# One gate multiply from GpSimd to VectorE behind a layer norm, and batch norm shifts issued among the statistics

## The chip, the cores and the metric

The kernel runs on one core of a Trainium2 chip. The metric is the device time of one execution in microseconds (us); lower is better. Times of whole executions spread over about 1 us and more from one execution to the next. So a second measure is used throughout, read from the traces: **the length of the passage**, from the first matmul of the first pointwise convolution behind attention to the first matmul of the second feed-forward block. All that the change touches lies in there.

## The reference, cut to what matters

A conformer block over x of 2 x 4000 tokens and 512 features: a feed-forward block, attention, a convolution module, a second feed-forward block, a last layer norm. The passage holds the end of attention and the convolution module:

```python
x2 = x1 + attn
h = _layernorm(x2, axis=-1)
h = h @ w_pw1
a = h[..., :D].copy()
b = h[..., D:].copy()
h = a * _sigmoid(b)                       # the gate
hp = jnp.pad(h, ((0, 0), (pad, K - 1 - pad), (0, 0)))
dc = jnp.zeros_like(h)
for i in range(K):                        # depthwise convolution, K = 3
    dc = dc + hp[:, i:i + T, :] * dw[i][None, None, :]
flat = dc.reshape(-1, D)                  # batch norm over ALL tokens
mu = flat.mean(0)
var = ((flat - mu) ** 2).mean(0)
dc = (dc - mu[None, None, :]) / jnp.sqrt(var[None, None, :] + 1e-05)
h = _silu(dc) @ w_pw2
x3 = x2 + h
```

The batch norm's mean and variance run over all 8000 tokens, so nothing of the second feed-forward block can start before the last chunk of tokens has left attention and gone through layer norm, pointwise convolution, gate, depthwise convolution and statistics. That makes the passage a chain.

## The kernel before

Tokens are worked in 16 chunks of 500 (`NCK`), four tiles of 125 in a chunk, features in 4 blocks of 128 (`DC`). `last` is chunk 15, `tail` is chunk 14. `KEEP` is 1. Most chunks' convolutions run beside attention; the passage does the rest. The gate of chunk `tail`:

```python
def conv_a(self, t, jj):
    ps, b_ps = self.pw1(t, jj)
    k, gs = jj % 2, t % 2
    out = self.G[gs][:, jj, 1:1 + CHUNK]
    wr = [self.b_G[gs][jj], self.b_Gl[gs][jj], self.b_Gr[gs][jj]]
    if t == NCK - 2 and jj >= self.KEEP:
        asb, b_asb = self.asb[jj % 3], self.b_asb[jj % 3]
        self.act(asb, ps[:, 0:CHUNK], AF.Copy, [b_ps], [b_asb], scale=2.0)

        def gate(eng):
            self.S.op(eng, lambda e: e.tensor_tensor(out=out, in0=asb, in1=self.th[k], op=ALU.mult), ...)
            self.halo_left(t, jj)          # one-column copies, on GpSimd
            self.halo_right(t, jj)

        if jj < DC - 1:
            return gate("POOL")
        return lambda: gate("DVE")
    elif t == NCK - 1:
        self.halo_left(t, jj)
        self.S.op("DVE", lambda e: e.scalar_tensor_tensor(...), ...)     # gate from PSUM
    # ... (the other chunks, and halo_right)
```

The layer norm that runs between, tile by tile. `ln_factor` ends with a power on GpSimd; `finish` prepares ScalarE's shift with a one-column instruction on VectorE, which is the profile's L620:

```python
def ln_tiles(self, c, sl, prepare=None, engs=("ACT", "ACT", "ACT", "DVE"), src=None):
    def finish(ti):
        if engs[ti] == "ACT":
            S.op("DVE", lambda e: e.scalar_tensor_tensor(               # L620
                out=self.sh[sl][:, ti:ti + 1], in0=self.mv[sl][:, ti, 0:1], scalar=-1.0,
                in1=self.rs[sl][:, ti:ti + 1], op0=ALU.mult, op1=ALU.mult), ...)
        self.ln_norm(c, sl, ti, self.ltm[ti][0:TILE, :], self.b_ltm[ti], engs[ti], src)

    for ti in range(TPC):
        if prepare:
            prepare(ti)
        if ti:
            self.ln_mean(sl, ti - 1)
        self.ln_stats(c, sl, ti, src)
        if ti:
            self.ln_factor(sl, ti - 1)
        if ti > 1:
            finish(ti - 2)
            yield ti - 2
    # ... (the last two tiles)
```

`depthwise(t, cc)` issues three matmuls into a PSUM bank and returns two functions: the statistics on VectorE (L1048) and the copy on ScalarE. `conv_scale(cc)` aggregates a block's statistics on VectorE (L1055) and takes the power on GpSimd (L1057); `conv_shift(cc)` multiplies mean and scale on VectorE (L1062); `swish` applies both on ScalarE. All waits are semaphores, placed by a helper that tracks each buffer's writers and readers. The order of the calls in the passage is shown in the diff below.

## Time and profile before

| | before |
|---|---|
| time, three first executions | 2060.94, 2061.27, 2062.01 us |
| span of the profile | 2056.9 us |
| TensorE busy | 2044.4 us (99%) |
| VectorE / ScalarE / GpSimd busy | 1111.3 / 744.6 / 128.1 us |
| length of the passage (1526.44 to 1564.25) | 37.81 us |
| TensorE idle in the passage | 0.95 + 0.23 + 0.12 + 0.85 + 0.32 + 0.87 = 3.34 us |

TensorE is the engine that sets the time, so only its idle times can be won. The prediction calls three of them gap A (0.95), gap B (0.23) and gap C (0.85) and says what each waits for.

### The profile page before, as it was taken

To read this page: it belongs to the slowest core of one execution; us is meant where nothing else is said; L and a number is where in the kernel's file an instruction comes from. 1 tells how busy PE (TensorE), PEld (TensorE's weight loads), DVE (VectorE), ACT (ScalarE), POOL (GpSimd) and SP (SyncE) were. 2 spreads that over 40 slices of the span, in tenths; PEclk is the share of its full clock that TensorE was granted. 3 is DMA by queue.
4 is the path that set the end of the run, shared out by engine and by line. 5 is a ranking of instruction groups with operands and counts; after the bars stand their busy time and mean duration, and the time that the engine had idled before them with its cause. 6 is when DMAs were issued, how large, how long until landed. Compare 5 with 4: busy or idle time off the path is not lost.

```text
span 2056.9 us, 24335 instructions
## 1 busy us (share of the span) xinstructions
PE 2044.4 (99%) x9625; PEld 1036.1 (50%) x9625; DVE 1111.3 (54%) x2274; ACT 744.6 (36%) x1270; POOL 128.1 (6%) x275
## 2 busy tenths in 40 slices
PE   9999999999999999999999999999999999999998
PEld 4555555554444444444444444444445555555554
DVE  4245444325556667666666676667764443443443
ACT  3433333333333333333333333333345443443432
POOL 2011100000000000000000000000011000000000
PEclk9999999999999999999999999999999999999999
DMA  7222221110000100014301000101143111111111
GB/s 178 56 61 56 58 61 49 46 49 11 16 6 23 24 16 18 21 23 110 92 17 24 18 23 14 23 18 24 39 127 93 31 31 41 31 31 41 31 31 42
DMA packets 209323, 87.71 MB, mean 43 GB/s; under 512 B 157873, under 2 KB 208692, under 8 KB 209204
## 3 DMA queue, kind: packets, MB, share of 16 engines
q1 hardware_dynamic: 208808, 85.79, 16.7%
q8 instruction: 77, 1.26, 0.3%
q14 instruction: 42, 0.34, 0.1%
q10 hardware_dynamic: 396, 0.31, 0.0%
HBM read 29.53 MB, written 19.04 MB: 24 GB/s over the span
## 4 chain that ended last, share of the span: by engine, by line
PE 96%; DVE 2%; SPq 1%; DMA 1%; issue 0%; POOL 0%; ACT 0%; POOLq 0%; DVEq 0%; ACTq 0%
PE s L465 54%; PE y L465 42%; SPq L515 1%; DMA xt<-in_x_dram 1%; DMA work<-in_dw_dram 0%; DVE work L547 0%; SPq L511 0%; DVE work L569 0%; DVE wff L1048 0%; DVE xt L667 0%; SPq L519 0%; POOL work L661 0%; POOL work L1057 0%; DVE wff L953 0%; ACT work L507 0%
## 5 line engine op out<-in xcount | busy, mean ns | idle before, releaser
L507 ACT ACTIVATE work<-s 128x500 bf16<-128x500 f32 (+2 forms) x1063 | 623.7, 587 | 1220.4 <-PE s L465 1218.9
L465 PE MATMUL s<-work,wff 128*128 128x500 bf16 x2560 | 627.7, 376 | 1.7 <-DVE work L504 1.7
L465 PE MATMUL s<-work,keys 128*128 128x500 bf16 x2048 | 517.5, 374 | 0.1
L465 PE MATMUL y<-work,keys 128*128 128x500 bf16 x2048 | 514.4, 373 | 0.1
L465 PE MATMUL y<-wff,work 128*125 128x512 bf16 x2016 | 506.6, 379 | 0.0
L820 DVE TENSOR_TENSOR work<-work 128x500 f32<-128x500 f32 x496 | 334.8, 675 | 281.9 <-ACT work L507 279.1
L465 PEld LDWEIGHTS s<-work,wff 128*128 128x128 bf16 x2560 | 250.1, 98 | 280.9 <-issue 1.8
L465 PEld LDWEIGHTS y<-wff,work 128*125 128x125 bf16 x2016 | 275.2, 137 | 173.5
L465 PEld LDWEIGHTS y<-work,keys 128*128 128x128 bf16 x2048 | 199.2, 97 | 234.4 <-DVE work L885 1.1
L465 PEld LDWEIGHTS s<-work,keys 128*128 128x128 bf16 x2048 | 199.8, 98 | 232.2 <-DVE work L749 0.6
L667 DVE SCALAR_TENSOR_TENSOR xt<-y,xt 125x512 bf16<-125x512 f32 x128 | 79.8, 684 | 342.0 <-PE y L465 342.0
L547 DVE BATCH_NORM_STATS2 work<-xt 125x6 f32<-125x512 bf16 x316 | 199.8, 681 | 10.4 <-DMA xt<-in_x_dram 10.2
L556 POOL TENSOR_TENSOR work<-work 125x4 f32<-125x4 f32 x76 | 77.0, 1013 | 1116.6 <-DVE work L554 1116.6
L465 PE MATMUL s<-work 128*125 128x512 bf16 (+3 forms) x528 | 133.7, 378 | 2.2 <-DVE work L1158 1.2
L569 DVE TENSOR_SCALAR work<-xt,work 125x512 bf16<-125x512 bf16 x279 | 113.0, 449 | 16.5 <-POOL work L556 12.9
L667 DVE SCALAR_TENSOR_TENSOR xt<-s,xt 125x512 bf16<-125x512 f32 x56 | 38.8, 692 | 146.3 <-PE s L465 146.3
L465 PEld LDWEIGHTS s<-work 128*125 128x125 bf16 (+2 forms) x528 | 70.5, 135 | 48.1 <-issue 2.7
L667 DVE SCALAR_TENSOR_TENSOR xt<-s,work,xt 125x512 bf16<-125x512 f32 x64 | 48.1, 751 | 32.5 <-PE s L465 31.9
L465 PE MATMUL s<-keys,work 128*128 128x500 bf16 x256 | 64.4, 376 | 0.0
L957 DVE SCALAR_TENSOR_TENSOR wff<-wff,s 128x500 bf16<-128x500 f32 x57 | 38.6, 678 | 43.5 <-PE s L465 41.4
L507 ACT ACTIVATE wff<-s 128x500 f32<-128x500 f32 x67 | 39.2, 587 | 57.2 <-PE s L465 55.1
L507 ACT ACTIVATE work<-keys,work 128x500 bf16<-128x500 bf16 x64 | 50.5, 795 | 1.1 <-DVE work L1062 1.1
(90 smaller groups left out, 491.4 us busy)
## 6 DMA issues: line engine op xcount, KB each, us to landing
xt<-in_x_dram SPq DMA_DIRECT2D x15, 500.0 KB
out_dram<-work SPq DMA_DIRECT2D x15, 500.0 KB
dcvd<-wff SPq DMA_DIRECT2D x52, 125.0 KB, 1.7
keys<-dcvd SPq DMA_DIRECT2D x13, 500.0 KB, 4.3
wff<-in_w_ff_a_dram SPq DMA_DIRECT2D x16, 256.0 KB, 4.7
keys<-work SPq DMA_DIRECT2D x8, 512.0 KB, 3.6
keys<-keys SPq DMA_DIRECT2D x32, 128.0 KB, 2.1
work<-work SPq DMA_TRANSPOSE x210, 2.5
```

The lines of the kernel that those rows point to most:

```text
L465: self.S.op("PE", lambda e: e.matmul(out, lhsT, rhs, start=start, stop=stop), reads=reads, writes=[bank], inc=stop if inc is None else inc)
L507: return self.S.op("ACT", lambda e: e.activation(out, in_, func, **kw), reads=reads, writes=writes)
L515: return self.S.dma("SP", k, lambda e: e.dma_start_transpose(dst, src), reads=reads, writes=writes)
L547: self.S.op("DVE", lambda e: e.bn_stats(self.st[sl][:, ti, :], x), reads=[b_x], writes=[self.b_st[sl][ti]])
L556: S.op("POOL", lambda e: e.tensor_tensor(out=self.rs[sl], in0=self.va[sl], in1=self.neghalf[0:TILE, :], op=ALU.pow), reads=self.b_va[sl] + ...
L569: self.S.op("DVE", lambda e: e.tensor_scalar(out, x, self.mv[sl][:, ti, 0:1], self.rs[sl][:, ti:ti + 1], ALU.subtract, ALU.mult), reads=[b ...
L667: self.S.op("DVE", lambda e: e.scalar_tensor_tensor(out=self.XT[g], in0=ps, scalar=scalar, in1=self.XT[g], op0=ALU.mult, op1=ALU.add), rea ...
L820: S.op("DVE", lambda e, p=p: e.tensor_tensor(out=self.acc[s], in0=self.acc[s], in1=self.P[p], op=ALU.add), reads=[self.b_P[p], self.b_acc[ ...
L957: self.S.op("DVE", lambda e: e.scalar_tensor_tensor(out=out, in0=self.th[k], scalar=1.0, in1=ps[:, 0:CHUNK], op0=ALU.add, op1=ALU.mult), r ...
```

## The change

Its intent: GpSimd is slow at the gate (1.245 us, against 0.672 on VectorE), so block 2's gate goes to VectorE, behind the layer norm, where block 3's already is. The depthwise convolution of chunk 13's block 2 reads what that gate's halo copies write, so it moves behind as well. And the shifts of the batch norm, which VectorE issued ahead of the next block's statistics, are issued between the two statistics.

```diff
@@ -945,7 +945,7 @@
                 self.halo_left(t, jj)
                 self.halo_right(t, jj)
 
-            if jj < DC - 1:
+            if jj < DC - 2:
                 return gate("POOL")
             return lambda: gate("DVE")
         elif t == NCK - 1:
@@ -1275,22 +1275,24 @@
             self.conv_b(tail, jj)
             self.conv_a(tail, jj)
 
+        gates = []
+
         def prepare(ti):
             self.project(last, ti)
             if ti == 0:
                 self.conv_b(tail, DC - 2)
-            if ti == 2:
-                self.conv_a(tail, DC - 2)
+            if ti == 1:
+                gates.append(self.conv_a(tail, DC - 2))
 
         for ti in self.ln_tiles(last, self.nxt("ln", self.LN_SLOTS), prepare, ("ACT", "ACT", "DVE", "DVE")):
             if ti == TPC - 3:
                 self.conv_b(tail, DC - 1)
-                gate = self.conv_a(tail, DC - 1)
+                gates.append(self.conv_a(tail, DC - 1))
         drains = [self.depthwise(tail - 1, self.KEEP)]
         for k in range(2):
             self.transpose_pair(k, 1, ("ACT", "DVE")[k], ybank())
-        drains.append(self.depthwise(tail - 1, DC - 2))
-        gate()
+        for gate in gates:
+            gate()
         self.load(self.Wp2, i["w_pw2"].rearrange("(c p) f -> p c f", p=128), [self.b_Wp2])
         for t in range(6, TCB):
             self.fetch_conv(t)
@@ -1304,6 +1306,8 @@
                 f, copy = self.depthwise(t, cc)
                 f()
                 copies.append(copy)
+                if t == last and cc > 1:
+                    self.conv_shift(cc - 1)
             self.conv_scale(cc)
 
         def copy_away():
@@ -1316,26 +1320,26 @@
                 self.act(self.nr1, self.onef, AF.Silu, [self.b_onef], [self.b_nr1])
             copy_away()
             self.conv_a(last, jj)
-            if jj > 1:
-                self.conv_shift(jj - 2)
+            if jj == 2:
+                self.conv_shift(0)
             if jj:
                 finish(jj - 1)
             else:
-                f, copy = self.depthwise(tail - 1, DC - 1)
-                f()
-                copies.append(copy)
+                for cc in (DC - 2, DC - 1):
+                    f, copy = self.depthwise(tail - 1, cc)
+                    f()
+                    copies.append(copy)
         self.swish(0, 0)
         self.swish(0, 1)
         copy_away()
         clear = (14848 - 12288) // (F // self.NWA * 2)
         for k in range(clear):
             self.load_wa(i["w_ff2_a"], k)
-        self.conv_shift(DC - 2)
-        self.swish(0, 2)
         all_t = range(TPC)
         banks = [self.sbank() for _ in all_t]
         self.pw2_x(0, all_t[0:2], banks[0:2])
         finish(DC - 1)
+        self.swish(0, 2)
         self.conv_shift(DC - 1)
         self.swish(0, 3)
         copy_away()
```

## The prediction

What the text on record said of the hardware that no trace of this case shows is cut from it, and the cuts are marked. The sum came to -0.29 + 0.64 - 0.72 = -0.37 us; L620 goes from 0.74 to 0.15 us once no gate runs on GpSimd beside it. That it does was the author's estimate, from two ends that agree to 0.01 us. The first rival is that GpSimd's gate was not what held L620.

> **What bounds the kernel now.** I first read the engine totals of the page: TensorE (PE) is busy 2044.4 of 2056.9 us, VectorE (DVE) 1111.3, ScalarE (ACT) 744.6, GpSimd (POOL) 128.1. The granted clock is 1.000. A change that moves VectorE and GpSimd work can only win what TensorE idles, 12.5 us in all, most of it at the first loads and the last store. Next come the waits of TensorE over the whole span (engine and line that waited, releaser, total us, times, longest us):
>
> ```profile
> PE s L465 <- DVE work L504: 1.7, 3, 0.9
> PE s L465 <- DVE work L1158: 1.2, 1, 1.2
> PE s L480 <- ACT work L507: 1.1, 2, 0.8
> PE y L493 <- ACT work L507: 1.0, 1, 1.0
> PE s L465 <- ACT work L507: 0.8, 1, 0.8
> PE y L493 <- DVE xt L504: 0.3, 1, 0.3
> ```
>
> L1158 and L480 lie elsewhere (weight folding, head). The rest is to be placed by the timeline of TensorE from 1524 to 1572 us, the passage between attention (its last matmul is at 1526 us) and the second feed-forward block. Its idle times are 0.95, 0.23, 0.85, 0.32 and 0.87 us, besides one of 0.12 us at 1550.8 that is worked out from two neighbouring lines; 3.34 us together. The change's code lies around these three:
>
> ```profile
> 1536.96 1.07 PE L493 MATMUL y<-work 125*128 125x125 bf16 x12 [0.95 <-ACT work L507]
> ...
> 1538.91 1.86 PE L465 MATMUL s<-work,wff 128*128 128x500 bf16 x8 [0.23 <-DVE work L504]
> ...
> 1556.30 1.08 PE L465 MATMUL s<-work 128*125 128x512 bf16 x4 [0.85 <-ACT work L507]
> ```
>
> Gap A (0.95): the transposes of layer-norm tile 1 wait for ScalarE's normalisation. Gap B (0.23): the first pointwise convolution of the last chunk waits for the copy of the transposed tiles. Gap C (0.85): the second pointwise convolution of chunk 0 waits for the last swish. The other two (0.32, 0.87) belong to the layer norm that follows gap C and start from its end, so they move with it.
>
> Why is gap A there? The timeline of all engines around 1534 us (start, us, engine, line, operation):
>
> ```profile
> 1533.29 1.25 POOL L943 TENSOR_TENSOR wff<-wff 128x500 bf16<-128x500 f32 x1 [0.21 <-ACT wff L507]
> ...
> 1533.80 0.74 DVE L620 SCALAR_TENSOR_TENSOR work<-work 125x1 f32<-125x1 f32 x1
> ...
> 1534.58 0.81 ACT L507 ACTIVATE work<-xt,work 125x512 bf16<-125x512 bf16 x1 [1.37 <-DVE work L620]
> ```
>
> L620 works on one column and takes 0.15 us in its other executions (median 151 ns of 7, longest 745). Here it lasts until 1533.80 + 0.74 = 1534.54, and GpSimd's gate multiply lasts until 1533.29 + 1.25 = 1534.54. VectorE stood still some 0.6 us for the gate. It is in the chain that ended last, which runs through VectorE from the third residual (1532.4) to the normalisations.
>
> Why gap C? The chain that ended last, from 1552 us:
>
> ```profile
> 1552.10 0.56 POOL work L1057
> ...
> 1552.75 0.09 DVE work L1062
> 1552.85 0.68 DVE wff L1048
> ...
> 1555.44 0.81 ACT work L507
> ...
> 1556.30 0.44 PE s L465
> ```
>
> L1057 is GpSimd's power for the scale of channel block 2, L1062 its shift on VectorE, L1048 the statistics of block 3. VectorE ended block 2's aggregate at 1552.02, then idled 0.73 us for the power before the shift, with block 3's statistics queued behind it. Block 3's first matmuls (1550.88, three of 0.213 us pitch) had been complete since about 1551.7.
>
> [...]L620 has two SBUF inputs and ends with the gate, while the neighbouring statistics (0.69 us, one SBUF input) and residuals (0.74 us, one input from PSUM) ran beside gates at their usual durations.[...] here the same gate takes 1.245 us on GpSimd and 0.672 us on VectorE, 1.85 times.
>
> **The change part by part.**
>
> 1. *Gate of block 2 from GpSimd to VectorE.* It takes 1.245 us from GpSimd, and adds one VectorE gate of 0.67 us (0.60 from start to start) after the copy of the transposed tiles, beside the gate of block 3 that is there already. [...]L620 goes from 0.74 to 0.15, worth about 0.59 us of VectorE's chain. But block 2's first half now precedes the third projection on TensorE, so that projection goes from about 1530.7 to 1531.58. Its last matmul ends at 1531.58 + 3 x 0.213 + 0.38 = 1532.60, and the residual, which started at 1532.37, starts at about 1532.68: 0.31 late. From there the old steps run: L620 at 1532.68 + 1.43 = 1534.11, the fourth residual at 1534.18 (was 1534.47), L620 of tile 1 at 1535.62 (was 1535.91), the normalisation to 1536.61, the transposes at 1536.67. **Minus 0.29 us**, and everything behind it, up to the copies that end gap B, shifts alike: the last chunk's convolution starts at 1538.62 in place of 1538.91.
>
> 2. *The depthwise of chunk 13's block 2 moves behind that convolution.* It needs the gate that now comes later. Before, its three matmuls filled 3 x 0.213 = 0.64 us between the transposes and gap B. Now TensorE idles there and does them later: gap B becomes about 0.23 + 0.64 = 0.87, and from block 1's convolution on TensorE is at 1538.62 + 1.71 + 1.28 = 1541.61 in place of 1541.26. **Plus 0.64, so plus 0.35 so far.** VectorE can take the gate: copy at 1537.78, gates 1538.38 and 1538.97, statistics to 1540.24; ScalarE's copy and sigmoid to 1541.34; last chunk's gate 0 to 1542.05, two statistics of 0.70 to about 1543.40, and gate 1 must wait for TensorE until about 1543.57 (1543.22 + 0.35). Spare: 0.17 us. From gate 1 on the chain is statistics, aggregate, power, halo copies, next gate, 3.2 us a round (1543.22, 1546.40, 1549.67), above TensorE's 14 x 0.213 = 2.98; it carries the 0.35 through unchanged.
>
> 3. *Shifts among the statistics.* The shift of block 2 now follows the first of block 3's two statistics. With 0.35 of lag: aggregate of block 2 at 1552.12, first statistics at 1552.35 to 1553.05, power ready by 1553.0, shift at 1553.10, second statistics at 1553.18 to 1553.88, aggregate at 1553.92, power at 1554.24, shift at 1554.89, swish 1555.09 to 1555.89, TensorE at about 1555.94 against 1556.30. One instruction of 0.70 now lies in a wait of 0.73: **minus 0.72**. Block 1's shift waits for nothing in either order: zero. The swish of block 2 has its shift at 1553.26 and ends, at 0.81 us, by 1554.1, ahead of its matmuls at 1554.6.
>
> Sum: -0.29 + 0.64 - 0.72 = **-0.37 us**. As gaps: A 0.66, B 0.87, C 0.85 - 0.72 = 0.13 plus what the other signs move; from 3.34 to about 2.97 us in all. No other part of the program changes. 2061.27 - 0.37 = **2060.9 us**.
>
> **Rivals.** [...] Against: both ends agree to 0.01 us. Then part 1 is a loss of 0.31 in place of a win of 0.29, and the sum is +0.23: 2061.5. *VectorE becomes the bound in front of gate 1.* For it: one more gate, and only 0.17 us spare[...]. A delay of 0.3 there goes straight into the chain: 2061.2. *TensorE was not going to need the earlier swish*, because it arrives late itself: its queue reaches the last four matmuls at about 1555.5 in the new schedule, so gap C can shrink by no more than some 0.1 beyond what I take: a floor of about 2060.8. *A loss is possible only* if two of these meet.
>
> **Range and chances.** The mechanism moves the time by -0.5 to +0.3. The three runs of before spread over 1.07 us, so the median of new runs can differ by half a microsecond and more without any cause. Both together give 2059.8 to 2062.2. Two per cent is 41 us, over ten times all TensorE idling in the passage: within 2% is all but certain.
>
> **What would show it right or wrong.** Right: no L620 above 0.2 us in the passage; the only large GpSimd gate at 1529; tile 1's transposes near 1536.7; a TensorE wait of about 0.9 us before the last chunk's convolution near 1538.6; block 1's convolution near 1541.6; no 0.73 us VectorE wait before L1062 of block 2; last swish near 1555.1 and a TensorE wait before it of 0.1 to 0.2. Wrong: a gate 0 or gate 1 delayed beyond TensorE's results (then the second rival), tile 1's transposes later than before (the first), or a swish of block 2 that TensorE waits for.

## The result, and the profile after

| | before | after |
|---|---|---|
| median, first comparison | 2061.34 (4 runs, 2060.94 to 2062.01) | 2060.18 (4 runs, 2059.99 to 2061.96) |
| median, second comparison | 2060.71 (8 runs, 2060.56 to 2061.84) | 2060.13 (5 runs, 2059.82 to 2061.94) |
| ratio, first; second | | 0.9996 [0.9979, 1.0013]; 0.9998 [0.9984, 1.0012] |
| passage | 37.81 us | 37.35 us, and 37.33 in a second trace |

A ratio is the mean time of one kernel's fast runs over that of the other's of the same rounds, so it isn't quite the ratio of the medians. By time alone the two kernels can't be told apart; the traces show the passage 0.46 us shorter. Of the 0.7 us between the two profiled spans (2056.9 and 2056.2), 0.18 is there before the passage starts (1526.44 and 1526.26), in code that the change doesn't touch.

The waits of TensorE in the changed kernel, over the whole span (engine and line that waited, releaser, total us, times, longest us):

```profile
PE s L465 <- DVE work L504: 2.3, 3, 0.9
PE s L465 <- DVE work L1158: 1.3, 1, 1.3
PE s L480 <- ACT work L507: 1.1, 2, 0.8
PE y L493 <- ACT work L507: 0.6, 1, 0.6
PE y L493 <- DVE xt L504: 0.3, 1, 0.3
```

The wait on ScalarE's swish (0.8, gap C) is no longer in the list. The one on the normalised tile (L493 on L507) fell from 1.0 to 0.6, and that on the copies (L504) rose from 1.7 to 2.3: gap C is no longer listed (0.26 us of it is left, which this view hides; see the third rival below), gap A is shorter, gap B longer. TensorE's timeline of the changed kernel places them (start, us, then what, and in brackets the idle time before it with its releaser):

```profile
1536.46 1.07 PE L493 MATMUL y<-work 125*128 125x125 bf16 x12 [0.63 <-ACT work L507]
1538.41 1.86 PE L465 MATMUL s<-work,wff 128*128 128x500 bf16 x8 [0.87 <-DVE work L504]
1540.11 1.43 PE L465 MATMUL y<-wff 128*128 128x500 bf16 x6
1541.37 1.86 PE L465 MATMUL s<-work,wff 128*128 128x500 bf16 x8
...
1552.70 4.04 PE L465 MATMUL s<-work 128*125 128x512 bf16 x16
```

Gap B grew to 0.87 because the three matmuls that used to stand in front of it are now among the six behind the convolution. In the last line all sixteen matmuls of the second pointwise convolution stand together. Before they were twelve and four, 0.85 us apart.

The timeline of all engines around 1534 us, where L620 stood still before:

```profile
1533.90 0.15 DVE L620 SCALAR_TENSOR_TENSOR work<-work 125x1 f32<-125x1 f32 x1
```

L620 is at 0.15 us. And the chain that ended last, at its end in the passage:

```profile
1552.15 0.56 POOL work L1057
...
1552.80 0.06 DVE work L1062
...
1552.91 0.70 DVE wff L1048
...
1554.81 0.81 ACT work L507
```

The same instructions as before, but only one of block 3's two statistics now stands behind the shift (L1062); the other ran while GpSimd worked. The last swish starts at 1554.81 in place of 1555.44.

Two lines of VectorE and GpSimd, taken from their own timelines, show something that cost nothing here but looks like what L620 met in the kernel before. VectorE's two gates:

```profile
1538.18 1.26 DVE L943 TENSOR_TENSOR wff<-wff 128x500 bf16<-128x500 f32 x2
```

and GpSimd's one-column halo copies behind the first of them:

```profile
1538.91 0.57 POOL L1027 COPY wff<-wff 128x1 bf16<-128x1 bf16 x1 [2.27 <-DVE wff L943]
1539.42 0.18 POOL L1037 COPY wff<-wff 128x1 bf16<-128x1 bf16 x1
```

The first copy takes 0.57 us where others take 0.18, and ends at 1539.48, just behind the second gate (1538.18 + 1.26 = 1539.44). It takes 0.57 in the three traces with both gates on VectorE whose list of GpSimd was read there (after, e2, e7), and 0.19 in the kernel before. So a long duration was seen on both sides: L620's 0.74 us beside GpSimd's gate, and this copy's 0.57 beside VectorE's second gate. Both lie in the reported duration and not in the idle time before it.

### The profile page after: what moved, and what is told of

It is laid out like the page before. It is cut to its first block, busy times and chain, and to the rows that moved or that the text cites. A ratio compares the mean times of both kernels' runs of the same rounds, so it can differ in the third digit from the quotient of the medians.

```text
span 2056.2 us, 24336 instructions
## 1 busy us (share of the span) xinstructions
PE 2044.3 (99%) x9625; PEld 1036.2 (50%) x9625; DVE 1112.1 (54%) x2275; ACT 744.7 (36%) x1270; POOL 127.0 (6%) x274
## 4 chain that ended last, share of the span: by engine, by line
PE 98%; DVE 1%; issue 0%; POOL 0%; ACT 0%; DMA 0%; POOLq 0%; SPq 0%; DVEq 0%; ACTq 0%
PE s L465 55%; PE y L465 42%; DVE work L547 0%; ACT work L507 0%; DVE wff L1048 0%; DVE work L569 0%; DMA xt<-in_x_dram 0%; POOL work L661 0%; POOL work L1057 0%; DVE xt L667 0%; DVE wff L953 0%; DVE work L504 0%; DVE work L654 0%; PE y L493 0%; DVE work L1055 0%
## 5 line engine op out<-in xcount | busy, mean ns | idle before, releaser
L507 ACT ACTIVATE work<-s 128x500 bf16<-128x500 f32 (+2 forms) x1063 | 623.8, 587 | 1220.0 <-PE s L465 1218.5
L507 ACT ACTIVATE wff<-s 128x500 f32<-128x500 f32 x67 | 39.2, 587 | 56.7 <-PE s L465 54.6
L507 ACT ACTIVATE work<-keys,work 128x500 bf16<-128x500 bf16 x64 | 50.5, 795 | 0.4 <-DVE work L1062 0.4
```

Of the source, the lines that this page charges most:

```text
L507: return self.S.op("ACT", lambda e: e.activation(out, in_, func, **kw), reads=reads, writes=writes)
```

## The experiments

All twelve runs gave correct results. e1 to e8 were executed once each, so whether they were in the fast state is unknown, and they are read by the passage of their traces and not by their times. Passage lengths, with the prediction for each:

| run | what it is | expected | passage |
|---|---|---|---|
| e1 | part 3 alone | 37.06 | 37.07 |
| e2 | parts 1 and 2 alone | 38.1 | 39.78; 38.10 without a clock drop |
| e3 | before, L620 with one tensor input | 37.35 | 37.35 |
| e4 | after, extra GpSimd multiply over L620 | 37.5 to 37.65 | 37.43 |
| e5 | after, GpSimd fills over L620 | 37.35 | 39.01; 37.33 without a clock drop |
| e6 | e1 and e3 together | 36.6 | 36.60 |
| e7 | after, early halo copies | 36.95 | 37.03 |
| e8 | e1, e3 and early halo copies | 36.2 | 36.28 |
| e9 | after, again | 37.35 | 37.33 |
| e10 | after, gap B filled | 37.35 | 37.33 |
| e11, e12 | e1 and e8, timed | 37.07, 36.28 | 37.04, 36.28 |

### e1: the shifts alone

```diff
 # finish(cc), in the kernel before
                 copies.append(copy)
+                if t == last and cc > 1:
+                    self.conv_shift(cc - 1)
             self.conv_scale(cc)
 # loop over jj
-            if jj > 1:
-                self.conv_shift(jj - 2)
+            if jj == 2:
+                self.conv_shift(0)
 # behind it
-        self.conv_shift(DC - 2)
-        self.swish(0, 2)
 ...
         finish(DC - 1)
+        self.swish(0, 2)
         self.conv_shift(DC - 1)
```

> The kernel before with only the shifts moved among the statistics (part 3). I measure the passage from the first matmul behind attention's last one to the first matmul of the second feed-forward block: 37.81 us before, 37.35 us after. My theory: part 3 is worth 0.75 us by itself, TensorE's wait before the last swish (0.85 us) falls to about 0.1, gaps A and B stay at 0.95 and 0.23: passage 37.06, shorter than the changed kernel's. Rival: the shift only pays together with the moved gate, because TensorE would not yet need the swish: passage 37.6 to 37.8.

Measured: 37.07 us, with gaps A and B at 0.95 and 0.23 as before, and the sixteen last matmuls in one piece of 4.04 us, as in the changed kernel. Part 3 is worth 0.74 us without any help from the moved gate, and by itself gives more than the whole change. The rival falls.

### e2: the moved gate alone

The reverse of e1's diff, applied to the changed kernel.

> The changed kernel with part 3 undone, so only the gate and the depthwise moved. My theory: L620 takes 0.15 us, gap A 0.63, gap B 0.87, gap C stays at about 0.85, so a loss of 0.29: passage 38.1 us against 37.81 before. Rival: the moved gate wins by itself[...]: passage 37.5 or less.

Measured: gaps 0.63, 0.87 and 0.85, L620 at 0.15: as the theory says. But the passage was 39.78 us, and TensorE's timeline shows a line that no other kernel had shown so far:

```profile
1538.85 3.44 PE L465 MATMUL s<-work,wff 128*128 128x500 bf16 x8 [0.87 <-DVE work L504]
```

Eight matmuls that took 1.86 us elsewhere took 3.44. The view by stretches of 1 us (stretch, its length, TensorE busy with its instructions, **granted clock**, share of DMA, GB/s) tells why:

```profile
1538.00:1539.00 1.00, 0.15 (x1) 0.97 1.01 323
1539.00:1540.00 1.00, 1.00 (x3) 0.50 0.92 312
...
1542.00:1543.00 1.00, 1.00 (x5) 0.82 0.00 0
```

From about 1538.95 to 1542.35, 3.4 us, the clock was halved. From the first of those eight matmuls to the next convolution took 4.64 us in this run and 2.96 in the changed kernel: a loss of 1.68. Without it the passage is 39.78 - 1.68 = 38.10, what the theory said (37.81 + 0.29). So the moved gate by itself loses 0.29 us, even though it frees L620. The clock drop is taken up below, with e9 and e10.

### e3: L620 without its second tensor input

```diff
-                S.op("DVE", lambda e: e.scalar_tensor_tensor(
-                    out=self.sh[sl][:, ti:ti + 1], in0=self.mv[sl][:, ti, 0:1], scalar=-1.0,
-                    in1=self.rs[sl][:, ti:ti + 1], op0=ALU.mult, op1=ALU.mult),
+                S.op("DVE", lambda e: e.tensor_scalar(
+                    self.sh[sl][:, ti:ti + 1], self.mv[sl][:, ti, 0:1],
+                    self.rs[sl][:, ti:ti + 1], -1.0, ALU.mult, ALU.mult),
```

> The kernel before, with L620 written as a multiply by two scalars (one SBUF tensor input in place of two); the gate stays on GpSimd and runs beside it. My theory[...]: the instruction takes about 0.15 us although the gate runs, VectorE's chain is 0.59 us earlier, but tile 1's power still stands behind the gate on GpSimd, so gap A goes from 0.95 to about 0.5 and the passage to 37.35 us; gaps B and C stay. Rival (any short VectorE instruction after a scalar factor is held up by a running GpSimd gate, or the instruction waited for something else): it takes 0.74 us again and the passage stays 37.8.

The same product; the scale is now a per-partition scalar and not a second tensor. The timeline around it:

```profile
1533.84 1.25 POOL L943 TENSOR_TENSOR wff<-wff 128x500 bf16<-128x500 f32 x1 [0.21 <-ACT wff L507]
...
1534.35 0.20 DVE L620 TENSOR_SCALAR work<-work 125x1 f32<-125x1 f32 x1
```

The gate ran from 1533.84 to 1535.09, and L620 ran in the midst of it, in 0.20 us (0.21 for tile 1, beside no gate). Gap A went to 0.56 and the passage to 37.35: the same win as the whole change, for one rewritten instruction.

### e4 and e5: GpSimd work over L620 that reads, and that doesn't

```diff
 # prepare(ti), in the changed kernel; e4, then e5
+            if ti == 2:
+                S.op("POOL", lambda e: e.tensor_tensor(out=self.asb[0], in0=self.asb[2], in1=self.th[0], op=ALU.mult), ...)
+            if ti == 2:
+                for _ in range(2):
+                    S.op("POOL", lambda e: e.memset(self.fill, 0.0), ...)     # 1000 fp32, over asb[0] and asb[1]
```

> The changed kernel with an extra gate-sized multiply on GpSimd (result not used) behind tile 0's power, to run at about 1532.9 to 1534.2 of this passage's clock, over L620's time at 1533.9. My theory: L620 lasts until the extra multiply ends, about 0.3 us in place of 0.15, and everything behind moves by 0.15 to 0.3: passage 37.5 to 37.65. Rival ([...]the old gate did harm only by delaying GpSimd's powers): L620 0.15, passage 37.35.

> The changed kernel with two extra fills of 1000 fp32 elements on GpSimd behind tile 0's power, in the same place as the extra multiply of the run before; a fill writes SBUF and reads nothing. [...]L620 takes 0.15 us while a fill runs, passage 37.35. Rival (any GpSimd work holds it): L620 lasts until a fill ends, passage 37.5 or more.

In e4 the extra multiply, at its own line L1282, and L620:

```profile
1533.20 1.24 POOL L1282 TENSOR_TENSOR wff<-wff 128x500 f32<-128x500 f32 x1
...
1534.23 0.23 DVE L620 SCALAR_TENSOR_TENSOR work<-work 125x1 f32<-125x1 f32 x1
```

L620 ended at 1534.46, just behind the multiply (1533.20 + 1.24 = 1534.44). It overlapped less than I had reckoned, so it was held 0.08 us and not 0.15 to 0.3, and the passage grew by the same 0.08. The size was missed, but L620 did last until the multiply ended. In e5 (one line more in the file, so L620 is L621 here):

```profile
1533.68 1.92 POOL L1284 MEMSET wff<- 128x1000 f32 x2
...
1534.73 0.15 DVE L621 SCALAR_TENSOR_TENSOR work<-work 125x1 f32<-125x1 f32 x1
```

Two fills ran from 1533.68 to 1535.60, and L620 took its 0.15 us from 1534.73 on, in the latter half of that time, beside the second. So L620 with two tensor inputs was held beside a GpSimd multiply, which reads SBUF (0.74 us before, 0.23 in e4), and wasn't held beside a fill, which reads nothing (0.15 in e5); with one tensor input it wasn't held beside the multiply either (0.20 in e3). What in the chip does this, no trace shows. e5's trace had the half clock as well: 4.64 us in place of 2.96 at the same spot, and 39.01 - 1.68 = 37.33 without it.

### e6, e7, e8: what is left

e6 is e1 and e3 in one kernel. e7 is the changed kernel with this edit; e8 has all three:

```diff
         elif t == NCK - 1:
-            self.halo_left(t, jj)
+            if jj < 2:
+                self.halo_left(t, jj)
+            if jj == 1:
+                self.halo_left(t, 2)
+                self.halo_left(t, 3)
```

> The kernel before with part 3 and with L620 written with one tensor input; gate and depthwise stay where they were. If the two gains add and part 2 of the change is a pure loss: gap A about 0.5, gap B 0.23, gap C about 0.1, passage 37.81 - 0.45 - 0.75 = 36.6 us, 0.75 shorter than the changed kernel. Rival: VectorE or ScalarE become the bound before the last swish and eat one of the two: 36.9 to 37.1.

> The changed kernel with the left halo copies of the last chunk's blocks 2 and 3 issued on GpSimd before block 0's power in place of behind it. My theory: the two VectorE idles of 0.93 us before gates 2 and 3 of the last chunk were waits for GpSimd's power and halo copy; they shrink until TensorE's own result is the bound, some 0.5 us over two rounds; the last swish comes 0.5 earlier and TensorE reaches it without a wait, winning the 0.4 it still waits: passage 36.95 us. Rival: those idles end with TensorE's or ScalarE's result, as the releaser names them, so nothing moves: 37.35.

> The kernel before with part 3, L620 with one tensor input, and the early halo copies. If the gains add: 36.6 - 0.4 = 36.2 us for the passage, 1.6 below before and 1.15 below the changed kernel. Rival: ScalarE's copies or VectorE's statistics take over as the bound in front of the last swish: 36.4 to 36.6.

e6: 36.60 us, the two gains add. e7 concerns two waits of VectorE, before the last chunk's gates 2 and 3. In the kernel before they read:

```profile
1546.40 0.68 DVE L953 SCALAR_TENSOR_TENSOR wff<-s,wff 128x500 bf16<-128x500 f32 x1 [0.93 <-ACT keys L507]
...
1549.67 0.68 DVE L953 SCALAR_TENSOR_TENSOR wff<-s,wff 128x500 bf16<-128x500 f32 x1 [0.93 <-POOL wff L1030]
```

The first names ScalarE as the releaser, the second GpSimd. The code has gate 2 wait for no such copy of ScalarE's, but for its own halo copy, which stood behind block 0's power in GpSimd's queue. With the halo copies issued early:

```profile
1547.20 0.68 DVE L957 SCALAR_TENSOR_TENSOR wff<-s,wff 128x500 bf16<-128x500 f32 x1 [0.72 <-PE s L465]
...
1550.18 0.68 DVE L957 SCALAR_TENSOR_TENSOR wff<-s,wff 128x500 bf16<-128x500 f32 x1 [0.64 <-PE s L465]
```

Both waits are shorter and both are now for TensorE. So the first releaser was misnamed. The win was 0.32 us and not 0.40, because no more was there to win: the last four matmuls now follow the others without a wait, although block 3's first statistics waited 0.28 us for TensorE's depthwise. The sixteen take 3.73 us, and sixteen of the same shape that wait for nothing take 3.62 (at 1558.03 in this trace); the 0.11 left is lost at the ninth and tenth, which wait for block 2's swish. e8: 36.28 against 36.2 expected, 1.53 us below before.

### e9 to e12: timed, and the half clock

e9 is the changed kernel unedited. e10 puts three matmuls into gap B whose result nobody reads; e11 is e1 and e12 is e8, for their times:

```diff
 # e10, in the changed kernel
         for gate in gates:
             gate()
+        self.warm(3)
```

> The changed kernel again, unedited. Two of the five traced executions with its order of work so far (the gate move alone, and the one with extra fills) showed TensorE's granted clock at 0.50 for 3.4 us, from just behind gap B on, at a loss of 1.6 to 1.7 us; no trace with the old order showed it. If the two close gaps (0.63 and 0.87 us within 2.4 us) bring this on, depending on where they fall, some of these executions are 1.7 us longer than the others at the same work, and the median of the rest is about 0.5 to 1 us below the kernel before. If it was chance on those two, all executions lie within about 1 us.

> The changed kernel with three matmuls whose result is not used in gap B (0.64 us of work between the transposes and the last chunk's convolution), where the moved depthwise used to be. The convolution still waits for the copy, so the passage should stay 37.35 us. If the long idle brings on the half clock, no execution of this kernel shows it and its spread is below 1 us; if chance, it shows it as often as the run before.

> Part 3 alone, timed: passage 37.07 in its trace, 0.74 below before and 0.28 below the changed kernel. Theory: 0.5 to 1 us faster than before, and no execution with the half clock, since gap B stays 0.23. Rival: the clock drops here too, because gap A is longer (0.95).

> Part 3, L620 with one tensor input and the early halo copies, timed: passage 36.28 in its trace, 1.53 below before and 1.07 below the changed kernel. Theory: 1.3 to 1.7 us faster than before (0.07%), fastest of the four[...].

| kernel | executions, us | median |
|---|---|---|
| before | 2060.56, 2060.56, 2060.61, 2060.68, 2060.74, 2060.79, 2061.39, 2061.84 | 2060.71 |
| e9, after | 2059.82, 2059.97, 2060.13, 2060.24, 2061.94 | 2060.13 |
| e10, after with gap B filled | 2060.26, 2060.36, 2060.37, 2060.56, 2060.62 | 2060.37 |
| e11, shifts alone | 2059.51, 2059.78, 2061.03, 2061.16, 2061.56 | 2061.03 |
| e12, all three | 2059.11, 2059.40, 2059.52, 2059.79, 2061.23 | 2059.52 |

No ratio to before leaves 1 by more than its interval (e12: 0.9995 [0.9981, 1.0009]). The changed kernel has two sets of times: with the first four runs, seven executions lie within 2059.82 to 2060.24, and two at 2061.94 and 2061.96, 1.9 us higher. That is near the 1.68 us of the half clock, but the record does not bear it out. Each execution's mean granted clock is on record. The 3.4 us at half clock of e2 and e5 take 0.0008 off the mean over 2059 us, so an execution that has them is at 0.999 at most, as e2 and e5 are; the one at 2061.96 is at 1.000. For the one at 2061.94 (0.999) it stays open, since a lower clock at the end of the span lowers the mean too (the profiled execution of the changed kernel has 0.999 without a drop in the passage: its clock is halved from 2052.80 us to the end, 2056.2). And long executions come without a long gap B: e12 has one at 2061.23, 1.8 us above the mean of its other four, e11 has three, 1.4 to 1.9 above its other two, and the kernel before has two in this table, at +0.7 and +1.2. One of e11's (2061.16) and both of before's are at 1.000. So something that was not found here makes executions long, and that none of e10's five was long says little of the clock. With gap B filled the passage was no longer (37.33, gap B's wait 0.23 again). e11's rival, that the clock drops there as well, is refuted for one of its long executions and open for two; e11's expectation in time was missed.

What is shown: two traces, e2 and e5, both with the long gap B, had the half clock for 3.4 us from just behind it (0.50 from 1538.94 to 1542.36 in e2, from 1539.72 to 1543.12 in e5, read from the view by stretches). The other four traces with a long gap B (after, e4, e7, e9) and all eight with a short one (before, e1, e3, e6, e8, e10, e11, e12) had 1.00 there. In the 3.41 us before the drop TensorE was busy for 1.84 us, in e2 and in e5; gaps A and B, 2.58 us from end to end, lie whole in them.

Why only these two had it was not found. In before and in after one stretch of full clock fills nearly the whole span; it lasts 2051.410 and 2047.997 us, which differ by 3.413, about as long as the half clock in e2 and e5. If the clock changes only at times that lie whole multiples of this apart, it matters how the two gaps fall on them: counted back from the end of the full clock in after (2052.80), such a time falls at 1537.39, between the two gaps, where the drops in e2 and e5 came 0.1 and 0.5 us behind both. In e4 (full clock to about 2054.1) it falls at about 1538.7, 0.1 us before the end of gap B, with TensorE busy for about 1.9 us of the 3.41 before it, hardly more than in e2 and e5, so e4 fits only narrowly. This is the author's estimate from these few stretches, and no run moved the gaps on purpose: it isn't tested. Nor is idle time alone what counts: behind TensorE's last matmul the clock was halved after 2.07 us in after (2050.73 and 2052.80) and after 4.86 in before (2051.37 and 2056.23), and in e1 and e7 it was still full 4.5 and 3.7 us behind it (at 2055.00).

e12 is the fastest of the five by its median, 1.19 us below before, against 1.53 in the passage and 1.3 to 1.7 expected.

## Why the prediction was right

The time was inside the range and the direction was right, but the measured medians differ by more than 0.37 us for reasons that aren't in the change (0.18 before the passage starts, and the spread of executions). The range also held the time of before, so the hit alone says nothing of the steps. They are judged by the traces, with each time counted from the start of the passage. Parts 1 and 2 were not run apart; their shares are read from the places in the trace.

- **Part 1, the shorter L620 and the later projection: -0.29 predicted, -0.32 measured** (1536.96 - 1526.44 = 10.52 before, 1536.46 - 1526.26 = 10.20 after). L620 at 0.15 and the third residual at 1532.45. The first rival, that GpSimd's gate wasn't what held L620, falls by e3, e4 and e5 (0.20, 0.23 and 0.15 us).
- **Part 2, the depthwise behind gap B: +0.64 predicted, +0.61 measured.** Block 1's convolution started at 14.82 before and 15.11 after, +0.29 with part 1, where +0.35 was predicted. Gap B is 0.87 as predicted. e2 shows parts 1 and 2 together as a loss of 0.29.
- **Part 3, the shifts: -0.72 predicted, -0.74 measured**, both in the changed kernel (the last swish at 29.00 before, 28.55 after, so -0.45, from +0.29) and alone in e1. Two small terms inside were off and cancelled in part. The shift of block 1 was said to be worth zero; it saves 0.08: from gate 3 to block 2's aggregate it takes 2.02 us in place of 2.10, because the second of two statistics of one block starts 0.71 us behind the first anyway, and the shift fits in between (1550.39 and 1551.10 with it, 1552.83 and 1553.54 before without it). And block 2's shift still waited 0.20 us for the power, because the first statistics began 0.17 us behind the aggregate and lasted 0.62, where I had reckoned 0.23 and 0.70.
- **The second rival, VectorE as the bound in front of gate 1,** didn't come about. The spare was 0.31 us and not 0.17: I had taken 0.70 us for each of two statistics, but two of different blocks take 1.26 together, and only two of the same block take 1.40. One of GpSimd's halo copies beside VectorE's gates did take longer (0.57 us in place of 0.18) and was covered.
- **The sum: -0.37 predicted, -0.46 measured.** No single term is off by more than 0.03; all three are off in the same direction.
- **The third rival,** a floor because TensorE comes late itself, was not reached in the changed kernel, and its size was wrong. I gave the last wait some 0.1 us of room to shrink further, although the prediction's own figures, TensorE's queue there at 1555.5 and the swish ready for it at 1555.94, are 0.44 us apart. The mistake was to read the room off the listed idle time. The listing counts from the modelled end of the matmul before (0.38 us), while these matmuls start 0.216 us apart, so it hides 0.16 us of a wait. Before, the first of the last four started 1.23 us behind its neighbour (1555.07 and 1556.30), so 1.01 late where 0.85 is listed. In the changed kernel it started 0.47 behind (1555.19 and 1555.66), so 0.26 late, where the view merges over the 0.10 not hidden and lists nothing; 0.1 to 0.2 was predicted. Of the sixteen's 4.04 us, 0.42 is lost against 3.62 without a wait: 0.31 at these last four, which e7 took, and 0.11 at the ninth and tenth, behind block 2's swish. That TensorE waits for this swish was on the list of signs of being wrong, but it is as much before the change.
- **Not foreseen:** the half clock, 1.68 us at a time, almost four times the gain. It was seen in e2 and e5, which share the longer gap B, and in neither of the two traces of the changed kernel itself. That this gap brings it on was not shown.

## What to carry to other kernels

Where GpSimd multiplies beside VectorE, look for a short two-input VectorE instruction whose duration is several times its usual one and ends with GpSimd's (0.74 us in place of 0.15 here, both ends at 1534.54); giving it one tensor input and a scalar won 0.46 us here, where moving the multiply and what hung on it lost 0.29. A value that another engine must first return is best issued behind the next independent piece of work of the same queue, as the shift behind the first statistics: before, VectorE idled 0.73 us ahead of the shift with the statistics queued behind it, and the new order alone won 0.74 us. Judge a change of half a microsecond in two milliseconds by places in the trace, and take a moved filler into account: what fills a gap of TensorE's is not free to move.
